# New emission orders for four stages of a convolution and attention kernel

## The chip, the cores and the metric

The kernel runs on one core of one Trainium2 chip. The metric is device time in microseconds (us) of one execution of the whole program; the time of a kernel is the median over several runs. A core has a matrix engine (TensorE, PE in the profile; its weight loads have a row of their own, PEld), a vector engine (DVE), a scalar engine (ACT), a further engine for simple fills (POOL), and an engine that here only issues transfers (SP). Each works through its own list of instructions in order, and waits at an instruction until its inputs and its output buffer are there. PSUM is the memory that PE writes; results are copied from it to SBUF by ACT or DVE.

## The reference

Four residual layers act on x, which has 2048 rows (positions) and 512 columns (channels), in bf16:

```python
x = A_u
x = x + _A_ref(_layernorm(x), A_re, A_im, B_re, B_im, C_re, C_im, log_dt, Dskip)
x = x + _B_ref(_layernorm(x), B_wqkv, B_wo)
x = x + _A_ref(_layernorm(x), ...)      # the same parameters again
x = x + _B_ref(_layernorm(x), B_wqkv, B_wo)
```

Layer A is a long convolution along the positions, one filter K per channel. K comes from a state-space model with 128 states n, and the convolution is done by Fourier transforms of twice the length:

```python
P = exp(logdA[:, :, None] * l[None, None, :])          # logdA = exp(log_dt) * (A_re + i A_im)
K = einsum("dn,dnl,dn->dl", Cc, P, dB).real            # dB = exp(log_dt) * (B_re + i B_im)
y = irfft(rfft(u padded) * rfft(K padded))[:L] + u * Dskip
```

Layer B is attention in a window: 32 heads of width 16, and each position looks at itself and at the 7 positions 2, 4, ... 14 before it:

```python
q, k, v = split(x @ wqkv)
logits = einsum("bhsd,bhswd->bhsw", q, k[idx]) * Dh ** -0.5     # w = 0..7, idx = pos - 2 w
o = einsum("bhsw,bhswd->bhsd", softmax(logits masked), v[idx])
return o @ wo
```

## The kernel before

The program runs in five stages, one for each entry of a list ORDERS: **prepare** (parameters, first layer norm), **first conv** (builds the filters and applies them), **B1** (first attention layer), **A2** (second convolution), **B2** (second attention layer).

**How a stage is ordered.** A stage doesn't emit its instructions at once. It records operations in a Plan, each with the engine it is for (P for PE, A for ACT, V for DVE, S for SP, G for POOL), a planner's duration, a function that emits the instructions, and the operations that must be emitted before it. Some steps exist in several ways, of which one is used (`either`): a sum on DVE, or by two identity matmuls on PE and a copy on ACT; a copy out of PSUM on ACT or on DVE (`moved`, lines 324 to 326); a transpose by DMA or on PE. `Plan.run` then emits the operations in the order of the numbers in ORDERS, taken as written, and a way is used if its numbers stand there:

```python
order = [int(i) for i in ORDERS[Plan.turn].split()]
Plan.turn += 1
taken = {self.ops[i][2] for i in order}
...
for i in order:
    fn, after, way = self.ops[i]
    fn()
```

So the numbers decide two things: for each engine the order in which it meets its work, and for some steps the engine. The planner's durations and due times were used where the numbers came from; nothing at run time reads them. The whole program is emitted under a manual schedule, so that nothing reorders it later.

**First conv, filters.** Channels are handled in 8 head groups (hc 0 to 7) for the filters and 4 channel blocks (dc 0 to 3, two head groups each) for the transforms. For a head group, DVE builds a table T of powers by doubling: at each level it multiplies the table by two multipliers (L386, L391, L392), and adds the two products. The sums of the larger levels are done on DVE (L399, L413) or on PE with ACT (matmuls L431 and L432, copy L436). The upper half of the table is made likewise (L407, L408: products; level 4: sum). Then three products with further factors (L456) give the right-hand sides: y0 and y1 in T's free parts, y2 in a tile of its own, Y2. PE contracts table and right-hand sides over the states (L469, L472: 256 matmuls for a head group, in eight pieces of 32), the result goes out of PSUM by ACT or DVE (L804) into KTq, to DRAM (k_scratch) and back in another layout (KT).

**First conv, transforms.** For the filters (kind k) and for the input (kind u), PE does the first Fourier step (L840), ACT copies it to Z (L845), Z is transposed to zt in four parts by DMA on SP's queue (or on PE, L871), PE does the second step (L860 to L863), and ACT copies the spectrum out (L867; tiles sp_u, sp_k). DVE multiplies the two spectra (L931, L932, tiles pa and pb); the halves are either joined on DVE (L936, L937), and then the inverse step has 8 matmuls, or not, and then it has 16 (L951 to L955). The result goes to VT by ACT or DVE (L959). A last step (L981) and a copy (L985) write the block of X. Filter spectra are stored for A2 (kt_scratch), also on SP's queue.

Buffers: T 2, Y2 1, pa and pb 2 each, zt and KTq together 4, spectra 8 of kind u and 4 of kind k, Z 1, and 3 for the PSUM tiles of sums and transforms, 2 for the contraction. An operation that takes the next buffer waits for the last reader of the one that it reuses.

**B1 and B2.** Norm and transpose of X (L153, xnT), projections to q and k (PE L1324; copies to qT and kT by ACT or DVE, L1329) and to v (L1344, L1349). For each of the 8 offsets, DVE multiplies qT with a shifted kT (L1375) and PE adds up each head with a matrix of ones (L1385). After the softmax DVE multiplies shifted values with the weights (L1487) and PE adds the offsets up with identity matmuls (L1503, L1508). The outcome is copied by ACT or DVE (L1523; L1525 for the last) and transposed. The output projection (L1560) is added to X either by DVE (L1543) or by an identity matmul ahead of it on PE (L1558) and a copy on ACT (L1656 with row sums, L1658 without). In B1 the next layer norm follows, with squares (L1664), a root (L174) and scaling (L1668, or L193 on DVE).

**A2** is first conv without the filters; spectra come back from kt_scratch.

Of the kernel before, what the change touches and what calls it, by code (L numbers as in the profile page):

```python
# [195 lines left out]
def load_params(nc, pp, prm):  # L196
# [13 lines left out]


ORDERS = [
    "297 1 3 2 7 5 8 21 9 25 10 20 24 22 11 12 225 15 13 29 229 26 14 27 33 233 31 23 41 34 237 44 46 37 43 50 249 47 "
    "51 231 38 58 245 60 57 235 61 48 241 298 59 227 68 299 72 74 253 239 77 300 75 84 251 69 88 85 90 247 99 303 76 "
    "91 98 243 304 106 104 307 255 114 107 115 308 120 136 320 124 258 256 132 259 137 125 108 109 257 92 139 93 260 "
    "138 261 122 321 123 146 262 154 156 263 158 133 291 152 293 279 269 159 287 155 276 301 168 166 164 302 322 169 "
    "167 174 323 175 182 184 305 180 324 306 185 325 183 191 190 311 200 201 309 207 198 196 310 312 206 199 264 313 "
    "212 219 317 218 213 314 272 326 288 282 315 294 266 274 327 284 316 270 280 328 141 296 140 147 319 318",
    "3 12 9 10 13 4 6 7 34 25 14 26 0 36 50 51 52 53 29 47 56 27 55 57 28 19 58 41 59 48 60 45 63 62 43 134 46 17 44 "
    "32 18 64 49 22 33 102 23 111 65 88 103 89 90 66 108 112 67 105 91 109 68 133 94 95 69 106 92 70 118 73 96 97 128 "  # L220
    "98 168 100 169 75 170 135 77 171 76 113 172 78 173 85 121 79 131 122 132 123 174 83 81 86 84 116 82 117 136 140 "
    "137 175 142 87 141 138 143 126 139 178 193 194 195 127 144 196 199 197 200 201 149 202 179 190 154 184 147 203 "
    "244 205 148 315 152 245 191 164 188 153 159 157 189 165 186 158 246 187 166 206 247 192 162 283 163 248 292 269 "
    "207 284 270 167 286 249 271 293 230 289 272 314 287 275 209 250 273 232 290 214 212 299 251 210 305 236 222 276 "
    "306 277 309 278 216 254 234 279 349 281 307 316 220 218 350 255 224 308 266 302 226 260 228 312 294 303 238 313 "
    "267 241 239 242 317 261 321 318 319 268 322 323 324 297 320 351 374 375 376 298 352 325 377 380 353 381 378 354 "
    "330 355 335 356 382 359 383 384 328 429 386 500 329 333 430 431 340 363 387 334 338 345 364 432 346 395 389 339 "
    "433 347 365 361 393 391 343 362 397 434 344 371 348 372 369 399 401 367 370 468 368 474 475 471 373 469 472 477 "
    "435 454 499 478 455 456 457 460 403 489 458 461 462 436 494 404 439 479 463 406 464 534 466 411 409 441 501 407 "
    "443 535 442 536 492 444 537 451 413 493 484 538 445 482 417 415 497 483 419 539 498 452 447 420 449 448 502 450 "  # L230
    "504 540 503 422 453 505 506 423 487 507 541 508 562 428 509 563 564 565 568 488 510 569 544 570 566 520 427 525 "
    "571 545 572 574 513 556 617 550 514 515 523 524 530 528 557 532 529 551 533 618 558 622 619 620 623 559 624 621 "
    "638 575 625 639 640 641 626 518 561 642 650 519 576 560 531 578 651 632 579 583 581 644 645 633 646 629 599 585 "
    "630 426 636 647 600 589 653 648 591 602 587 654 425 663 603 605 592 634 665 594 635 676 656 597 637 666 596 657 "
    "677 607 667 684 669 608 610 685 670 614 659 613 611 679 660 615 672 616 682 662 680 687 692 673 688 700 675 694 "
    "690 701 696 703 698 705 706 717 708 718 711 709 714 712 715",
    "58 1 59 39 2 3 20 40 4 41 21 60 11 10 22 7 23 5 16 24 13 26 17 42 28 32 43 14 47 194 30 61 49 35 104 68 195 62 "
    "66 79 64 105 54 45 76 81 75 101 78 197 102 51 82 199 72 85 84 107 86 228 110 108 229 112 113 244 88 115 248 245 "
    "89 119 246 249 230 120 247 94 232 122 252 233 231 250 123 96 253 234 124 251 97 91 236 254 235 92 237 116 256 "
    "258 257 255 118 259 163 242 240 98 164 238 241 100 243 239 144 260 132 145 264 262 133 278 263 265 126 274 284 "  # L240
    "279 127 135 285 275 272 136 160 129 286 161 266 273 130 138 287 268 267 139 154 288 147 269 276 155 151 289 157 "
    "270 152 277 290 159 271 291 169 280 296 179 170 332 172 176 180 340 185 177 333 334 186 341 182 338 335 183 191 "
    "200 344 339 192 148 346 345 149 188 336 347 189 141 342 201 337 142 166 297 343 167 173 348 305 298 174 301 350 "
    "306 351 365 302 352 379 366 282 205 353 283 307 380 206 202 319 354 367 308 203 355 320 368 356 214 321 357 369 "
    "217 215 299 370 218 358 211 359 300 375 212 208 364 376 373 209 220 226 223 303 221 227 374 224 311 304 309 312 "
    "385 310 377 313 316 393 315 378 386 395 318 394 399 396 389 400 322 390 371 323 372 397 381 324 383 387 398 384 "
    "391 325 388 429 326 392 430 331 404 407 401 406 415 408 403 413 416 409 414 431 410 419 523 432 411 420 524 433 "
    "521 417 434 412 421 522 418 437 438 422 439 440 527 423 441 525 426 442 425 448 528 443 452 526 428 449 456 497 "
    "529 450 531 453 446 533 457 454 532 451 444 447 530 455 463 534 461 498 445 535 465 462 464 536 473 541 466 459 "
    "501 543 469 537 474 460 475 503 467 502 471 539 470 472 504 479 476 468 493 480 477 499 485 489 481 494 500 490 "  # L250
    "491 486 549 505 483 508 487 507 484 550 545 509 562 488 506 546 492 482 510 553 564 561 495 511 563 589 512 565 "
    "554 517 590 566 595 572 519 604 567 591 513 605 574 608 571 596 516 586 606 610 597 587 569 619 559 588 618 621 "
    "607 560 620 609 622 573 611 612 623 575 613 624 576 616 626 577 614 578 628 581 579",
    "0 5 1 14 15 2 7 8 9 4 10 6 12 11 3 13 17 21 105 109 18 23 106 25 111 29 26 33 31 113 34 117 121 114 119 37 39 "
    "123 38 193 197 45 195 48 199 201 42 49 205 202 51 124 59 206 52 133 60 81 62 53 208 82 70 55 63 217 57 281 84 71 "
    "64 127 282 73 136 68 285 211 67 137 169 85 286 220 214 74 170 139 86 130 221 75 172 90 147 88 140 79 289 78 148 "
    "141 173 290 101 144 174 145 150 102 158 176 179 95 151 159 293 223 96 152 294 161 98 154 296 242 156 224 99 92 "
    "162 243 253 93 245 225 254 302 163 246 229 227 305 256 231 165 167 308 299 232 257 247 309 234 258 251 311 249 "
    "330 262 260 341 235 331 312 180 342 333 319 181 186 320 334 236 187 189 344 240 183 190 239 313 184 345 264 322 "
    "317 346 315 265 323 276 350 267 272 348 277 324 273 335 328 279 326 268 337 339 269 275 361 358 362 355 359 271 "  # L260
    "352 356 353",
    "1 20 2 3 58 21 4 22 59 39 12 8 9 23 60 40 16 5 24 13 26 17 41 30 32 42 61 14 28 194 62 68 35 43 101 64 195 45 66 "
    "104 102 49 51 47 79 105 54 76 80 126 77 75 85 127 72 82 86 107 83 228 88 108 229 90 91 230 110 92 232 94 112 244 "
    "231 233 113 96 236 97 245 114 119 234 248 237 120 235 246 249 116 122 250 252 247 117 251 242 98 240 243 99 253 "
# [1462 lines left out]
```

## Time and profile before

| what | us |
|---|---|
| five runs | 517.34, 518.18, 519.84, 521.27, 521.65 |
| median | 519.84 |
| the profiled execution | 521.86 |
| its span (first to last instruction) | 520.1 |
| prepare / first conv / B1 / A2 / B2, by where the tiles of one end and the next begin | 57 / 162 / 123 / 48 / 130 |
| granted clock of PE, mean | 0.962 |

The page of the profile gives busy time of each engine, slices of the span (a digit is a busy share in tenths), the DMA queues, the chain of work that ended last, and groups of like instructions. A row of a group has the line in the kernel, the engine, the operation, output and input tiles with their shapes, the count, busy time and the mean of one in ns, and the idle time just before them with what ended it. The view of busy time by stretches has for each stretch its length, then busy time and instruction count for PE, weight loads, DVE, ACT and POOL, then PE's granted clock, the share of time that the DMA engines were busy, and GB/s. The view of waits sums, for an engine at a tile and line, what it waited for: total, number, longest. "issue" there means that nothing which the profile shows held the instruction back. The timeline lists start, duration, instruction, and in brackets idle time ahead of it and what ended it.

### The profile page before, as it was taken

What the parts mean: (1) busy time and instruction counts of PE and PEld (TensorE: products, weight loads), DVE (VectorE), ACT (ScalarE), POOL (GpSimd) and SP (SyncE); (2) the same over time, 40 slices, a digit from 0 to 9 for tenths busy, and PEclk for the clock granted to TensorE, in tenths of its full rate; (3) what the DMA queues carried; (4) which work ended last, traced back from release to release, by engine and by line L of the source; (5) the groups of instructions that cost most, each with busy time, mean ns of one, the idle gap of its engine ahead of it and who ended that gap; (6) DMA issues with size and microseconds to landing.
All of it is one profiled execution on the core that took longest, in us unless ns stands there. A gap on an engine that the chain in (4) does not pass through costs nothing.

```text
span 520.1 us, 12435 instructions
## 1 busy us (share of the span) xinstructions
PE 419.2 (81%) x5208; PEld 245.4 (47%) x5224; DVE 474.9 (91%) x808; ACT 326.3 (63%) x482; POOL 13.0 (3%) x63
## 2 busy tenths in 40 slices
PE   1600678689778879899999879879997999998896
PEld 1500554367455548543355434556674434563353
DVE  6999999979997999789999999889999498999995
ACT  4999677658575758742655336989996546551320
POOL 0000000000000002200000000000000000000000
PEclk9999998979897969999999999989999999999999
DMA  8940464664664362651010622479510700203233
GB/s 258 164 169 1 82 115 112 126 131 94 116 141 114 52 155 68 202 106 47 16 59 28 112 40 40 113 253 182 71 36 0 122 30 20 83 24 88 42 75 148
DMA packets 105389, 49.87 MB, mean 96 GB/s; under 512 B 90619, under 2 KB 97532, under 8 KB 105076
## 3 DMA queue, kind: packets, MB, share of 16 engines
q1 hardware_dynamic: 104900, 48.67, 41.9%
q8 instruction: 41, 0.67, 0.5%
q10 hardware_dynamic: 432, 0.39, 0.2%
q14 instruction: 16, 0.13, 0.1%
HBM read 15.78 MB, written 8.13 MB: 46 GB/s over the span
## 4 chain that ended last, share of the span: by engine, by line
PE 40%; DVE 30%; ACT 11%; issue 8%; DMA 7%; SPq 4%; POOL 0%; DVEq 0%; ACTq 0%
PE ps_qk L1324 11%; DVE prod L1487 5%; PE ps_v L1344 5%; PE Lp L1385 4%; DMA zt<-Z 3%; DVE ln_st_b L153 3%; SPq L646 3%; DVE Ttab L456 2%; DVE Y2tab L456 2%; DVE prod L1375 2%; ACT Z L845 2%; PE psk L469 2%; DVE Ttab L392 2%; PE ps_o L1560 2%; PE po L1503 2%
## 5 line engine op out<-in xcount | busy, mean ns | idle before, releaser
L1375 DVE TENSOR_TENSOR prod<-qT,kT 128x2048 bf16<-128x2048 bf16 (+1 forms) x80 | 76.8, 1005 | 7.5 <-ACT kT L1329 6.0
L1487 DVE TENSOR_TENSOR prod<-VX,L 128x2048 bf16<-128x2048 bf16 (+2 forms) x96 | 77.3, 860 | 1.2 <-PE po L1508 0.7
L1324 PE MATMUL ps_qk<-xnT,wqk 128*128 128x512 bf16 x256 | 62.6, 382 | 0.0
L1503 PE MATMUL po<-prod,sb_ident 128*128 128x512 bf16 x215 | 54.7, 379 | 4.8 <-DVE prod L1487 2.9
L1324 PEld LDWEIGHTS <-wqk 128*128 128x128 bf16 x256 | 22.3, 98 | 30.9 <-issue 10.2
L1503 PEld LDWEIGHTS <-sb_ident 128*128 128x128 bf16 x224 | 21.0, 97 | 32.7 <-issue 9.0
L840 PE MATMUL ps_s<-X,sb_F 128*128 128x128 bf16 x128 | 12.2, 259 | 27.4 <-ACT X L669 25.5
L1344 PE MATMUL ps_v<-wv,xnT 128*128 128x256 bf16 x256 | 33.0, 278 | 1.2 <-ACT xnT L1302 1.0
L840 PEld LDWEIGHTS <-sb_F 128*128 128x128 bf16 x256 | 17.2, 108 | 33.7 <-issue 25.8
L1385 PE MATMUL Lp<-prod,sb_bones 128*32 128x512 bf16 x256 | 28.3, 388 | 4.6 <-DVE prod L1375 4.6
L456 DVE TENSOR_TENSOR Ttab<-Ttab,MPA 128x2048 bf16<-128x2048 bf16 (+2 forms) x20 | 28.4, 1433 | 3.0 <-ACT Ttab L436 2.8
L472 PE MATMUL psk<-Y2tab,Ttab 128*32 128x48 bf16 x1024 | 22.3, 199 | 10.2 <-issue 9.7
L845 ACT CAST Z<-ps_s 128x1024 bf16<-128x1024 f32 (+1 forms) x32 | 28.9, 996 | 1.7 <-DMA zt<-Z 0.9
L1349 ACT CAST VX<-ps_v 128x512 bf16<-128x512 f32 x31 | 18.2, 586 | 18.1 <-PE ps_v L1344 18.1
L1344 PEld LDWEIGHTS <-xnT 128*128 128x128 bf16 x256 | 24.0, 99 | 9.2 <-issue 4.0
L1560 PE MATMUL ps_o<-wo_t,oT 128*128 128x512 bf16 x108 | 27.7, 379 | 0.5 <-DVE X L1543 0.2
L456 DVE TENSOR_TENSOR Y2tab<-Ttab,MPB 128x6144 bf16<-128x6144 bf16 (+1 forms) x13 | 27.2, 2118 | 0.3 <-PE psk L472 0.3
L1523 ACT CAST ot<-po 128x1024 bf16<-128x1024 f32 x13 | 12.6, 1015 | 23.1 <-PE po L1503 21.1
L469 PE MATMUL psk<-Ttab 128*32 128x64 bf16 x1024 | 22.6, 204 | 5.3 <-DVE Ttab L456 2.8
L472 PEld LDWEIGHTS <-Ttab 128*32 128x32 bf16 x1024 | 19.8, 99 | 13.0 <-issue 12.8
L1329 ACT CAST kT<-ps_qk 128x512 bf16<-128x512 f32 x25 | 14.6, 585 | 16.8 <-PE ps_qk L1324 16.8
L153 DVE BATCH_NORM_STATS2 ln_st_b<-X 128x6 f32<-128x128 bf16 (+2 forms) x80 | 22.9, 354 | 2.1 <-ACT X L985 2.1
(231 smaller groups left out, 1031.3 us busy)
## 6 DMA issues: line engine op xcount, KB each, us to landing
X<-in_A_u_dram SPq DMA_DIRECT2D x8, 512.0 KB, 5.7
kt_scratch<-sp_k SPq DMA_DIRECT2D x16, 256.0 KB, 3.6
Kt<-kt_scratch SPq DMA_DIRECT2D x16, 256.0 KB, 6.3
out_dram<-X SPq DMA_DIRECT2D x4, 512.0 KB, 2.7
k_scratch<-KTq SPq DMA_DIRECT2D x7, 256.0 KB, 2.7
KT<-k_scratch SPq DMA_DIRECT2D x7, 256.0 KB, 2.9
VX<-VX SPq DMA_DIRECT2D x4, 448.0 KB, 3.8
kT<-kT SPq DMA_DIRECT2D x8, 192.0 KB, 2.1
```

What stands on the lines that cost most here:

```text
L153: self.nc.vector.bn_stats(self.st[:, j, part, :], X[:, j, a:b])
L456: nc.vector.tensor_tensor(d, src.to_broadcast([128, c, n, 2 * EYB]), mm.to_broadcast([128, c * n, EYB, 2]), ALU.mult)
L469: nc.tensor.matmul(o.rearrange("e (s i) -> e s i", s=2), xs, T[:, 1:3, h, m // 2, :, t], start=(m == 0), stop=False, skip_group_check=True)
L472: nc.tensor.matmul(o[:, EYB:].rearrange("e (q i) -> e q i", q=3), xs, Y2[:, :, h, 1 - m // 2, :, t], start=False, stop=(m == 3), skip_grou ...
L845: nc.scalar.copy(box["Z", kind, dc][:, 0:n // 8, :, jq * 32:(jq + 1) * 32].rearrange("p g r k -> p r g k"), box.pop(("s1", kind, dc, jq))[ ...
L1324: nc.tensor.matmul(ps[:], wqk[:, ct, f0:f0 + 128], xnT[:, 4 * s:4 * s + 4, ct, :], start=(ct == 0), stop=(ct == 3))
L1344: nc.tensor.matmul(ps[:, jj].rearrange("p t h d -> p (t h d)"), xnT[:, j + jj, ct, :], wv[:, ct, fp * 256:(fp + 1) * 256], start=(ct == 0) ...
L1375: nc.vector.tensor_tensor(pr[:, 0:n2], qT[fp][:, a:a + n2, j0 * 128:j0 * 128 + 1024], kT[fp][:, a:a + n2, c0:c0 + 1024], ALU.mult)
L1385: nc.tensor.matmul(Lp[r0:r0 + 32, w // 4, :], bones[:, w % 4, :], pr[:, f2 - a, hb * 512:(hb + 1) * 512], start=(n == 1), stop=(n == 4), s ...
L1487: nc.vector.tensor_tensor(p2[:, 0:nj].rearrange("p j t d h -> p (j t) d h"), VX[:, fp, NV + a:NV + a + nj].rearrange("p j (t d h) -> p (j ...
L1503: nc.tensor.matmul(po[:, c:c + 512], ident[:], p2[:, k + j:k + j + 2].rearrange("p j t d h -> p (j t d h)"), start=(n == 1), stop=(n == W))
L1560: nc.tensor.matmul(ps, box["oT"][:, ft // 2, j, ft % 2, :], wo_t[:, ft, :], start=(ft == 0 and not res), stop=(ft == 3))
```

## The change

Only the first four entries of ORDERS are replaced: those of prepare, first conv, B1 and A2. No function changes, no tile, no pool; the entry of B2 stays. Both kernels record the same operations under the same numbers, so an order that names other numbers takes another way.

```diff
 ORDERS = [
-    "297 1 3 2 7 5 8 21 9 25 10 20 24 22 11 12 225 15 13 29 229 26 14 27 33 233 31 23 41 34 237 44 46 37 43 50 249 47 "
...
+    "297 1 3 2 7 5 8 20 9 25 10 21 24 22 11 12 225 15 13 29 229 26 14 27 33 237 31 23 41 34 233 44 46 37 43 50 253 47 "
...
-    "3 12 9 10 13 4 6 7 34 25 14 26 0 36 50 51 52 53 29 47 56 27 55 57 28 19 58 41 59 48 60 45 63 62 43 134 46 17 44 "
...
-    "137 175 142 87 141 138 143 126 139 178 193 194 195 127 144 196 199 197 200 201 149 202 179 190 154 184 147 203 "
-    "244 205 148 315 152 245 191 164 188 153 159 157 189 165 186 158 246 187 166 206 247 192 162 283 163 248 292 269 "
...
+    "3 9 6 10 4 7 39 12 40 37 13 38 34 0 41 50 14 51 52 53 56 54 57 29 58 59 47 24 42 49 60 168 62 48 134 17 32 18 19 "
...
+    "81 84 154 82 144 246 87 149 159 157 247 248 193 158 194 249 195 196 250 199 166 197 200 147 222 152 148 251 162 "
+    "153 164 206 201 163 202 165 254 208 167 203 349 205 315 283 350 210 255 286 316 284 351 287 266 212 289 352 260 "
...
```

In words, the numbers come to this.

| stage | what changes engine | what changes place |
|---|---|---|
| prepare | nothing | a few neighbouring copies and products swap |
| first conv | two table sums of 128x2048 from PE and ACT to DVE, that is 16 fewer matmuls L431/L432 and 4 fewer copies L436; two pairs of joins from DVE to longer inverse steps (8 more matmuls each of L953 and L954); of KTq one copy and of its last part (KTu) one from DVE to ACT, of VT one from ACT to DVE | head group 3 is built before 2 (before: 2, then 3); contractions are emitted in pieces between transforms; the products of channel blocks 0, 1 and 2 go 2,0,3,1 / 3,0,2,1 / 2,0,1,3 (before 0,3,1,2 / 0,1,2,3 / 0,1,3,2); the four transposes of a filter spectrum are issued ahead of its stores |
| B1 | four copies to kT (L1329), one copy to ot (L1523) and one copy-like residual step each for two row blocks (L1543, replaced by L1558 and L1658) from DVE to PE and ACT; one norm from ACT to DVE | the first row blocks' statistics and projections, some products |
| A2 | one copy of VT from DVE to ACT | a few copies |

At channel block 0 the order of first conv is now as follows, in the numbers of the diff: 154, 144, 149, 159 are the four transposes of the filter spectrum on SP; 157, 147, 152, 162 the second Fourier steps of these parts on PE, and 158, 148, 153, 163 their copies on ACT; 193 to 196 and 199 to 202 the eight pieces of the contraction of head group 2 on PE, of which six stand between 157 and 147; 222, 206 and later 230, 214 the products on DVE; 208 the inverse step of the second of them. Before, 144, 149, 154 came first, the stores 164 and later 165, 166 among them and 159 behind 164, and the eight pieces stood ahead of 147.

## The prediction

> **What bounds the kernel now.** I read the page first, then busy time by stage, then the waits, then the instructions around the longest waits. The page says which engines can set the end:
>
> ```profile
> span 520.1 us, 12435 instructions
> PE 419.2 (81%) x5208; PEld 245.4 (47%) x5224; DVE 474.9 (91%) x808; ACT 326.3 (63%) x482; POOL 13.0 (3%) x63
> ...
> PEclk9999998979897969999999999989999999999999
> ...
> q8 instruction: 41, 0.67, 0.5%
> ```
>
> DVE (VectorE) is busy 474.9 of 520.1 us, so only 45 us in the whole span can be won without taking work off it. Queue q8 brings TensorE's instructions: 10,432 of them in 41 packets of 16 KB, one packet for about 254.
>
> The stages in one row each (length; busy us and instruction count of PE, weight loads, DVE, ACT, POOL; granted clock; DMA share; GB/s). They are prepare, first conv, first attention layer (B1), second conv (A2), second attention layer (B2):
>
> ```profile
> 0.00:57.25 57.25, 15.20 (x368) 12.55 (x368) 52.79 (x102) 49.32 (x79) 0.75 (x10) 1.00 0.55 134
> 57.25:219.00 161.75, 130.82 (x2926) 87.70 (x2928) 148.44 (x208) 108.89 (x139) 7.47 (x13) 0.91 0.56 121
> 219.00:342.00 123.00, 112.51 (x739) 54.86 (x746) 113.86 (x207) 67.81 (x117) 2.39 (x20) 1.00 0.31 70
> 342.00:390.00 48.00, 44.66 (x413) 32.50 (x411) 44.39 (x93) 44.48 (x67) 0.00 (x0) 0.96 0.61 120
> 390.00:520.10 130.10, 116.01 (x772) 57.80 (x776) 115.44 (x202) 55.76 (x83) 2.39 (x20) 0.98 0.26 63
> ```
>
> In the first conv DVE leads clearly (148.4 of 161.75, so 13.3 idle); PE and ACT have 31 and 53 us to spare, and only their lateness at a hand-over costs anything. In B1 DVE and PE are level. In A2 three engines lie within 0.3. The waits (engine, tile, line, what released it; total, times, longest):
>
> ```profile
> PE psk L472 <- issue: 9.7, 4, 3.9
> PE xp L860 <- DMA zt<-Z: 6.1, 3, 3.9
> ...
> DVE pa L931 <- PE vp L955: 3.0, 2, 2.5
> ...
> DVE Ttab L456 <- ACT Ttab L436: 2.8, 1, 2.8
> ...
> DVE pa L931 <- ACT sp_k L867: 1.9, 3, 0.9
> ```
>
> The three DVE rows are the visible cost, 7.7 us, and the PE rows are where they begin:
>
> ```profile
> 135.38 0.20 PE L472 MATMUL psk<-Y2tab,Ttab 128*32 128x48 bf16 x3 [2.26 <-issue]
> ...
> 137.30 0.63 PE L862 MATMUL xp<-zt,sb_C 128*128 128x512 bf16 x1
> ```
> ```profile
> 157.89 0.23 PE L472 MATMUL psk<-Y2tab,Ttab 128*32 128x48 bf16 x4 [3.94 <-issue]
> ```
> ```profile
> 163.53 1.23 DVE L456 TENSOR_TENSOR Ttab<-Ttab,MPA 128x2048 bf16<-128x2048 bf16 x1 [2.83 <-ACT Ttab L436]
> ```
>
> PE stands 3.94 us inside a contraction with nothing to wait for but instructions; the sums queued behind it finish late; ACT's copy L436 is late; DVE waits 2.83.
>
> **The change, part by part.** Only emission orders of four stages move; counts below are from the orders of the two kernels.
>
> *Prepare.* Same operations on the same engines, neighbours swapped. DVE is busy 52.79 of 57.25 and waits at the start for loads that do not move: 0 (bounds -1 to +1).
>
> *First conv, work.* Two more sums of 128x2048 (L399, 1.22 us each) on DVE: +2.4. Two pairs of joins L936/L937 (0.42 each) leave it for longer inverse matmuls: -1.7. Copies: two fewer of KT halves, one more VT (0.69): -0.7. DVE net 0.0. PE loses 16 sum matmuls and gains 16 of 128x256 (-16x0.43+16x0.27 = -2.6); ACT loses four copies L436 (1.02 each) and nets one KT copy: -3.5. Neither pays directly with 31 and 53 us spare.
>
> *First conv, waits removed.* I counted the DVE work standing between a PE/ACT sum's last input and DVE's first use of its result, in start-to-start times of the same instructions in the trace (1.14 for a 128x2048 one whose row says 1.22). Before, the shortest are 2.14 and 2.33 us, and those two gave 0.43 and 2.83. After, the shortest is 3.46, and the one nearest to a late contraction has more than 4. A sum takes 8x0.21 on PE and 2x1.02 on ACT, partly overlapped, about 3.0; so they should vanish: -3.3. Two waits of spectrum products for their spectra (0.92, 0.35), one for Y2 (0.34) and the product wait behind the 3.90 us transpose (2.53) also stand at places that the new order undoes: -4.1. Gone: 7.4.
>
> *First conv, waits added.* (a) The first spectrum product of channel block 0 follows the issue of its DMA transposes after 5.41 us of DVE work. Before, 6.11 and 5.92 gave waits of 0.92 and 0.35. So 0.9 to 1.6: 1.2. What is late next: the inverse matmuls, then pa's buffer. (b) The second product's transform stands on PE behind six of eight contraction pieces. With one fetch gap of 2 us its cover of 7.2 falls short by 0.8 to 2.8: 1.8. (c) PE itself waits for the first transpose: its landing takes 4.1 us (median of 42) plus the issue, DVE's work in between is only 2.85, so PE idles 1.3 to 3; behind it on PE stand the pieces of contraction 2 and the other transforms, for which ACT's copies and DVE's products wait, which is (a) and (b). [...] In the trace, after the 2.26 us gap at 135.38 the 128x512 matmuls start every 0.43 instead of 0.21 us until 139.0, and the granted clock of 130 to 140 is 0.83. [...] By the row, 8 matmuls at +0.21 follow it: 1.7, of which I take 0.7, since contraction pieces, which run at the pace of fetches, stand between. [...] (d) Products write two buffers of pa; one product of the last block stands 2.62 us behind the one whose buffer it reuses, with 4.3 needed: 1.7 (before, 3.28 against 3.57 gave 0.51). (e) Y2 has one buffer. The table of head group 5 is written directly when DVE reaches it, 7.45 us after contraction 4 may begin; that takes 4.0 to 4.7 and its fetch gap 0 to 3.9: wait 0 to 1.2, I take 0.6. DMA issues on SP keep their number; the k transposes now go out ahead of the stores of the kernel spectrum, which were hidden. POOL's fills of the tables follow their table and POOL is busy 7.5 of 161.75: 0. Added: 6.0. First conv: -7.4 + 6.0 = -1.4; bounds -6 (fetches fall well) and +5.
>
> *B1.* Four casts L1329 (0.69) go to ACT, where one takes 0.585; DVE is 27.5 busy of 33 us there (229 to 262) while PE is at 32.45, so PE hides most: of 2.8 I take -0.9, for the cast at the head of DVE's stretch and part of the product waits. One cast L1523 (1.22) goes to ACT (1.0), and two residual sums L1543 (0.68) become PE identity matmuls (0.38) and ACT copies (0.57); one norm of 0.40 comes to DVE. From 262 to 327 DVE is 62.71 of 65 busy and every microsecond counts, but from 327 to 342 ACT is 13.86 of 15, PE 14.12, DVE 13.73, and ACT takes up to 2.1 more. Of 2.2 I take -1.0. B1: -1.9; bounds -4.6 (all of DVE's saving) and +2.1 (ACT's tail on the path).
>
> *A2.* One VT copy goes from DVE (0.69) to ACT (0.60) with DVE, ACT and PE level: 0, bounds -1 and +1. *B2.* Same order: 0; it only starts earlier or later.
>
> Sum: -1.4 - 1.9 = -3.3. The profiled run took 521.86 us, span 520.1 plus 1.8 around it: it would become 518.6. It lies 2.0 above the median of the five runs, 519.84; I carry the difference over: 516.5.
>
> **Rivals.** *Full gain:* contractions spread between transforms give the fetches time, (b), (c) and (e) vanish (-3.1), and B1 gives its -3: 516.5 - 3.1 - 1.1 = 512.3. For: contraction pieces now alternate with transforms, which issue slower. Against: a contraction has two fetches whatever the order.
>
> *Nothing in B1, half in the conv:* PE paces B1 (112.51 against 113.86 tells how little), its tail gives back the rest, the conv gives -0.7: 519.1. That the orders don't matter, since data dependencies rule, ends here too; against it stand waits that the order alone makes.
>
> *Slower: the fetch in contraction 2.* The second product of block 0 hangs on a transform behind six pieces of that contraction. If a 3.94 us fetch gap falls there rather than 2, and the transforms that follow run at half clock (four of four matmuls, 16x0.21 = 3.4, not 0.7), its wait is 1.8 + 1.9 + 2.7 = 6.4; the pa buffer and Y2, whose covers are short or nil, pass it on instead of absorbing it, about 2 more. +6.6 on 516.5: 523.1. For: the 157.89 row did just this with a cover of 2.33. Against: 7.2 of cover. It decides once PE comes 5.9 us later than in my sum (519.84 + 2.6 - 516.5).
>
> **How the numbers follow.** A measurement of this kernel tells about 0.5%, 2.6 us. Chances: my case 0.40, full gain 0.13, no change 0.13, slower 0.34 (it has the largest single price, and new short covers tend to come where a count like mine doesn't look). Mine spans 513.5 to 519.5: of its 0.40, 0.29 is faster, 0.09 same, 0.02 slower. So faster 0.42, same 0.22, slower 0.36. Likeliest 516.5; 8 in 10 from 511.5 to 526.5, the lower end just past the full gain, the upper one past the slower rival by the +3.4 left of its bounds.
>
> **What would show it.** DVE's busy time falls by 4 to 6 us, nearly all in B1. The 2.83 and 2.53 waits are gone; waits of 0.9 to 2 stand at the products of block 0 and one in the last block; Y2's wait is at most 1.2. B1 is 1 to 3 us shorter, A2 and B2 within 1. Wrong: a first conv longer than 164 us, or DVE waits for PE of over 3 us in it; B1 no shorter though DVE is less busy in it; B2 different by over 2 us.

## The result: 0.6% faster, and not where the sum had it

| kernel | median us | runs | profiled execution us (span) |
|---|---|---|---|
| before | 519.22 | 76 | 521.86 (520.1) |
| changed | 515.74 | 41 | 513.88 (512.1) |

The ratio is 0.9939 with a 95% interval of 0.9926 to 0.9952, which is -3.2 us, or -2.5 to -3.8. The prediction's sum was -3.3. The two profiled executions stand 8.0 us apart, because that of before lies above its median and that of the changed kernel below: one profile of each doesn't give the size, and second profiles of both were taken with the experiments.

From the page of the changed kernel:

```profile
span 512.1 us, 12435 instructions
PE 409.8 (80%) x5211; PEld 239.2 (47%) x5226; DVE 469.3 (92%) x798; ACT 327.5 (64%) x486; POOL 13.0 (3%) x63
...
q8 instruction: 41, 0.67, 0.6%
```

DVE is busy 5.6 us less, as forecast (4 to 6); 4.0 of it is in B1, where nearly all was expected, 0.7 in first conv and 1.0 in A2. The stages, with their ends moved to the same work as before (columns as before):

```profile
57.25:211.70 154.45, 120.87 (x2931) 83.41 (x2930) 147.72 (x205) 105.86 (x135) 7.49 (x13) 0.96 0.58 127
211.70:334.90 123.20, 113.50 (x735) 54.59 (x741) 109.82 (x204) 71.47 (x124) 2.39 (x20) 1.00 0.30 74
334.90:382.10 47.20, 43.92 (x418) 31.40 (x418) 43.34 (x89) 45.04 (x68) 0.00 (x0) 1.00 0.59 110
382.10:512.10 130.00, 115.74 (x769) 57.61 (x774) 115.38 (x202) 55.63 (x83) 2.39 (x20) 0.98 0.26 63
```

First conv is 154.45 us long where it was 161.75, with 0.7 us less DVE work: it lost waits. B1 is 123.2 where it was 123.0, although DVE is busy 4.0 us less in it (109.82 after 113.86): what left DVE there came back as waiting. The waits say the same:

```profile
PE xp L860 <- DMA zt<-Z: 7.1, 6, 3.2
...
PE psk L469 <- issue: 6.0, 3, 2.6
PE psk L472 <- issue: 5.0, 2, 2.5
...
DVE prod L1375 <- ACT qT L1329: 4.2, 1, 4.2
...
DVE pa L931 <- ACT KTu L1009: 2.0, 1, 2.0
```

The rows for sums (L456 on L436) and for inverse steps (L931 on vp) are gone, so DVE lost 5.8 us of waits there and got one of 2.0. TensorE's instruction stalls are not gone: 11.0 us by these two rows, against 12.3 us of such gaps before. In B1 one wait of 4.2 us for qT is new.

### The profile page after: what moved, and what is told of

It reads as the page before. It is cut to its first block, busy times and chain, and to the rows that moved or that the text cites. A ratio compares the mean times of both kernels' runs of the same rounds, so it can differ in the third digit from the quotient of the medians.

```text
span 512.1 us, 12435 instructions
## 1 busy us (share of the span) xinstructions
PE 409.8 (80%) x5211; PEld 239.2 (47%) x5226; DVE 469.3 (92%) x798; ACT 327.5 (64%) x486; POOL 13.0 (3%) x63
## 4 chain that ended last, share of the span: by engine, by line
DVE 41%; PE 32%; ACT 9%; issue 8%; DMA 5%; SPq 3%; POOL 0%; DVEq 0%; ACTq 0%
PE ps_qk L1324 11%; PE ps_v L1344 5%; DVE prod L1487 4%; DVE Ttab L456 4%; DVE Y2tab L456 4%; PE Lp L1385 4%; DVE ln_st_b L153 3%; DVE Ttab L392 3%; DVE Ttab L399 3%; SPq L646 3%; DVE Ttab L391 2%; DVE prod L1375 2%; PE po L1503 2%; DVE Ttab L408 2%; DVE Ttab L407 1%
## 5 line engine op out<-in xcount | busy, mean ns | idle before, releaser
L840 PEld LDWEIGHTS <-sb_F 128*128 128x128 bf16 x256 | 16.9, 108 | 31.8 <-issue 24.5
L840 PE MATMUL ps_s<-X,sb_F 128*128 128x128 bf16 x128 | 10.8, 241 | 26.2 <-ACT X L669 24.7
L1523 ACT CAST ot<-po 128x1024 bf16<-128x1024 f32 x14 | 13.6, 1015 | 26.0 <-PE po L1503 26.0
L456 DVE TENSOR_TENSOR Ttab<-Ttab,MPA 128x2048 bf16<-128x2048 bf16 (+2 forms) x20 | 28.4, 1433 | 0.2
L1329 ACT CAST kT<-ps_qk 128x512 bf16<-128x512 f32 x29 | 17.0, 585 | 17.8 <-PE ps_qk L1324 17.8
L456 DVE TENSOR_TENSOR Y2tab<-Ttab,MPB 128x6144 bf16<-128x6144 bf16 (+1 forms) x13 | 27.2, 2120 | 0.0
L469 PEld LDWEIGHTS <-Ttab 128*32 128x32 bf16 x1024 | 19.1, 100 | 16.4 <-issue 15.6
L472 PE MATMUL psk<-Y2tab,Ttab 128*32 128x48 bf16 x1024 | 21.2, 197 | 5.2 <-issue 5.0
```

The source lines that it names most:

```text
L456: nc.vector.tensor_tensor(d, src.to_broadcast([128, c, n, 2 * EYB]), mm.to_broadcast([128, c * n, EYB, 2]), ALU.mult)
L469: nc.tensor.matmul(o.rearrange("e (s i) -> e s i", s=2), xs, T[:, 1:3, h, m // 2, :, t], start=(m == 0), stop=False, skip_group_check=True)
L840: nc.tensor.matmul(o, F1[:, j, r, :], rhs(j), start=True, stop=not dk)
```

## Experiments

The expectations name two theories: P is the sum of the prediction, C is what the two profiles suggest. All intervals are against the kernel before on the same chip. "Stage end" below is the start of B1's own first statistics, which wait for one of the last four copies of X out of first conv; "rest" is from there to the end.

### Which stage's order pays

Only the first two strings of ORDERS are the new ones (x1_conv):

```diff
-    "297 1 3 2 7 5 8 21 9 25 10 20 24 22 11 12 225 15 13 29 229 26 14 27 33 233 31 23 41 34 237 44 46 37 43 50 249 47 "
...
+    "297 1 3 2 7 5 8 20 9 25 10 21 24 22 11 12 225 15 13 29 229 26 14 27 33 237 31 23 41 34 233 44 46 37 43 50 253 47 "
...
-    "3 12 9 10 13 4 6 7 34 25 14 26 0 36 50 51 52 53 29 47 56 27 55 57 28 19 58 41 59 48 60 45 63 62 43 134 46 17 44 "
...
+    "3 9 6 10 4 7 39 12 40 37 13 38 34 0 41 50 14 51 52 53 56 54 57 29 58 59 47 24 42 49 60 168 62 48 134 17 32 18 19 "
...
```

> New orders of prepare and first conv, old orders of B1 and A2. Theory P (the sum of the prediction): -1.4 us against the kernel before. Theory C (the profiles: first conv carries all, B1 gives nothing because TensorE paces its head): the whole difference of the medians, -3.0 to -3.7 us, and a first conv without DVE waits above 0.5 us between 60 and 195 us.

Only the third string is new (x2_b1); prepare, first conv and A2 keep their old ones:

```diff
-    "58 1 59 39 2 3 20 40 4 41 21 60 11 10 22 7 23 5 16 24 13 26 17 42 28 32 43 14 47 194 30 61 49 35 104 68 195 62 "
...
+    "39 58 40 1 59 20 2 3 41 21 60 4 42 22 12 7 5 23 9 13 24 16 26 14 28 32 30 47 17 197 43 45 35 49 104 61 199 66 "
...
```

> New order of B1 alone. Theory P: -1.9 us. Theory C: within 0.5 us of the kernel before; DVE is busy about 4 us less in B1 and waits about 4 us more, in one wait of over 3 us at the first product of queries and keys.

The first two strings and the fourth are new, B1's is old (x3_conv_a2):

```diff
-    "0 5 1 14 15 2 7 8 9 4 10 6 12 11 3 13 17 21 105 109 18 23 106 25 111 29 26 33 31 113 34 117 121 114 119 37 39 "
...
+    "5 1 0 9 4 10 3 2 13 6 15 7 11 14 12 8 17 21 105 109 18 23 106 25 111 26 29 33 30 35 113 117 39 114 121 119 37 "
...
```

> New orders of prepare, first conv and A2, old order of B1. Theory P: the changed kernel without B1's gain, so 1.9 us slower than it and -1.4 us against before. Theory C: as fast as the changed kernel within 0.6 us, -3.0 to -4.3 us against before.

The changed kernel again, and in the next round the kernel before again, without an edit:

> The changed kernel once more, for a second profile of it beside the others. Theory C: -3.5 us against before; the span of the second profile lies within 3 us of 512.1 and first conv again shows no wait of DVE for sums. If the profiled pair's 8.0 us came from one odd execution of the changed kernel, the span is near 516 and waits of 1 us or more are back in first conv.

> The kernel before once more, for a second profile. If the profiled pair (span 520.1 against 512.1) overstates the change because the profiled execution of before was a slow one, this span is 515 to 518 and its waits for sums (2.83 us) and for the inverse step (2.53 us) are smaller or elsewhere; if they belong to the order, they are there again at the same instructions within 1 us.

And, after these, B1 and A2 both new behind the old first conv (z1_b1_a2), that is, the third and the fourth string:

> Old orders of prepare and first conv, new orders of B1 and A2. B1's new order alone came out 3.3 us slower. If its cost is real and its own, this is 1 to 4 us slower than before, and the time from the first statistics of B1 to the end is 301.5 to 303.5 us in the profile (old orders: 299.8 to 301.2). If A2's new order was made to follow it and pays it back, 0 within 1 us. Theory P: -1.9 us.

| kernel | median us (before beside it) | ratio, 95% interval | stage end | rest |
|---|---|---|---|---|
| before, first profile | | | 218.9 | 301.2 |
| before, second (y1) | 517.96 (519.09) | 0.9983, 0.9950 to 1.0015 | 216.2 | 299.8 |
| changed, first profile | 515.74 (519.22) | 0.9939, 0.9926 to 0.9952 | 211.6 | 300.5 |
| changed, second (x4) | 515.78 (518.97) | 0.9939, 0.9910 to 0.9968 | 212.5 | 303.3 |
| first conv new (x1) | 515.63 (518.97) | 0.9953, 0.9923 to 0.9982 | 212.1 | 301.7 |
| first conv and A2 new (x3) | 516.54 (518.97) | 0.9970, 0.9942 to 0.9998 | 212.2 | 301.9 |
| B1 new (x2) | 522.63 (518.97) | 1.0063, 1.0031 to 1.0096 | 219.6 | 302.2 |
| B1 and A2 new (z1) | 523.47 (519.36) | 1.0073, 1.0047 to 1.0098 | 220.1 | 301.9 |

First conv's new order carries the gain. By the median x1 is within 0.2 us of the changed kernel, as theory C has it. The times alone don't decide: x1's interval (-0.9 to -4.0 us) also holds theory P's -1.4, and x3 (-1.6, from -0.1 to -3.0) fits P as well. The traces do. No DVE wait above 0.3 us stands in x1's first conv before one of 1.40 at 195.4 us, and with the new order the stage ends at 211.6 to 212.5 us, with the old one at 216.2 to 220.1. The second profile of the changed kernel has a longer span than expected, 515.7 us; its first conv is nearly as short as in the first, 212.5 us.

B1's new order gives nothing: with the new first conv the rest is 300.5 and 303.3 us, against 301.7 and 301.9 with B1's old order. Behind the old first conv it even costs 3.3 and 3.8 us in two kernels, and most of that is the seam between two strings that were not made for each other. The end of first conv's string says in which order the last four parts of X are copied out: parts 3, 0, 1, 2 (numbers 718, 709, 712, 715) in the old one, 2, 3, 1, 0 in the new one. B1's string begins with the statistics of part 3 (number 58) in the old one, of part 2 (39) in the new one. So in the kernel before, as in the changed one, DVE starts after the first of the four copies; with B1 alone new it starts after the fourth:

```profile
218.24 1.91 ACT L985 CAST X<-ps_y 128x512 bf16<-128x512 f32 x3 [0.69 <-PE ps_y L981]
218.86 0.87 DVE L153 BATCH_NORM_STATS2 ln_st_b<-X 128x6 f32<-128x128 bf16 x4 [1.93 <-ACT X L985]
```
```profile
217.00 2.57 ACT L985 CAST X<-ps_y 128x512 bf16<-128x512 f32 x4 [0.69 <-PE ps_y L981]
219.60 0.87 DVE L153 BATCH_NORM_STATS2 ln_st_b<-X 128x6 f32<-128x128 bf16 x4 [3.92 <-ACT X L985]
```

That is 2.0 us more of waiting (3.92 for 1.93) in x2 and z1, and 0.7 (2.60) in x1 and x3, where DVE starts after the second copy. Less these 2.0 us, the old first conv ends at 217.6 and 218.1 us in x2 and z1, inside the 216.2 to 218.9 of before: it is not longer. The other 1.3 and 1.8 us agree with the rest, which is about 1.5 us longer than in the two profiles of before (300.5 on average). A2's new order, in z1, doesn't pay it back.

The second profile of before has the same two large waits at the same instructions as the first (2.53 and 2.83 us there), so they belong to the order:

```profile
112.54 0.69 DVE L931 TENSOR_TENSOR pa<-sp_u,sp_k 128x1024 bf16<-128x1024 bf16 x1 [2.22 <-PE vp L955]
```
```profile
161.14 1.23 DVE L456 TENSOR_TENSOR Ttab<-Ttab,MPA 128x2048 bf16<-128x2048 bf16 x1 [2.45 <-ACT Ttab L436]
```

By the two profiles of each kernel, first conv is 5.5 us shorter and the rest 1.4 longer, together -4.1 beside -3.5 by the medians.

### Taking one wait away

In the kernel before, the one sum in front of the 2.83 us wait is made on DVE (440) instead of by two steps on PE (441, 443) and two copies on ACT (442, 444); operations between these are left out here:

```diff
 # first conv, head group 6, level 3
-439 441 443 442 444 451
+439 440 451
```

> The kernel before with one sum of head group 6 (level 3, the one with 2.33 us of DVE work between its inputs and its use) made on DVE instead of TensorE and ACT, in the place where DVE waited for it. Cover theory: the wait of 2.83 us goes, 1.14 us of DVE work comes, -1.7 us. Rival (the wait is only where some slack of the stage shows, and comes back elsewhere): 0 to +1.2 us.

Measured: ratio 1.0006, interval 0.9984 to 1.0027; the rival's value. The wait is gone and the stage ends at 217.6, inside the range of the old order. A new wait of 0.88 us (for X) stands at 173.6, and one for a filter spectrum at 193.4 is 1.04 us, where the first profile of before has 0.60. Removing the largest wait of the list, one place alone, was worth nothing that could be measured.

### Does the new order stand lateness better?

> The kernel before with 64 matmuls of each of the eight contractions issued twice (the first of an accumulation, started anew, so the values stay): 128 instructions more, about 1.3 us of TensorE's issue time for each contraction, 10 us in all, in a stage where TensorE has 31 us to spare. Cover theory: this kernel, with covers of 2.1 to 3.3 us at its sums and products, loses 4 to 10 us.

> The changed kernel with the same doubled matmuls. Cover theory: with covers of 3.5 us and more it takes part of the lateness, loses 1 to 4 us, and stands 5 us or more ahead of the other one. If the new order merely moved work off TensorE or lost its stalls, both lose alike (difference within 1.5 us of 3.5).

```diff
 # Tables.contract
+if m == 0:
+    nc.tensor.matmul(o.rearrange("e (s i) -> e s i", s=2), xs, T[:, 1:3, h, 0, :, t],
+                     start=True, stop=False, skip_group_check=True)
 if m % 2 == 0:
     nc.tensor.matmul(o.rearrange("e (s i) -> e s i", s=2), xs, T[:, 1:3, h, m // 2, :, t],
```

Before with the extra matmuls: 526.06 us, ratio 1.014 (1.008 to 1.020). Changed with them: 527.16, ratio 1.0183 (1.0133 to 1.0233). The old order lost 1.4% (7 us, as expected), the changed one 2.4% of before's time (over 11 us, where 1 to 4 were expected), and its lead was gone. That speaks against longer covers as what the change brought: an order that stood lateness better would have kept its lead. But the edit also adds 1,024 instructions, 128 for each contraction, which by the step of 256 between stalls (last section) move the later fetches, and so these two runs don't separate lateness from the places of fetches.

### Moving the fetches and nothing else

The last test leaves both orders as they are and moves the places in TensorE's list at which a new block of instructions begins. 64 tiny matmuls are started twice in prepare, at a time when TensorE waits for other engines (18.8 us ahead of its first L840 in the first profile of before); with their weight loads that is 128 instructions, half a block of 256 (the step between stalls in the table of the last section):

```diff
 # prepare, sums of the rows of X
 for j in (j2 * 2, j2 * 2 + 1):
+    for _ in range(8 if j2 < 4 else 0):
+        nc.tensor.matmul(rows[:, j:j + 1], xT[:, j, 0, :], ones[:, 0:1], start=True, stop=False, skip_group_check=True)
     for ct in range(4):
         nc.tensor.matmul(rows[:, j:j + 1], xT[:, j, ct, :], ones[:, 0:1], start=(ct == 0), stop=(ct == 3), skip_group_check=True)
```

> The kernel before with 64 tiny matmuls (128 instructions with their weight loads, half of one fetch) started twice in prepare, where TensorE waits 22 us for other engines. Nothing moves but the places in TensorE's list at which a new fetch begins. If stalls of fetching set the waits of first conv (the 3.9 us one inside a contraction ahead of the 2.8 us wait of DVE), stalls move to other instructions and the time changes by 1.5 us or more, most likely down. If the order alone sets them: within 1 us of before, the same waits at the same instructions.

> The changed kernel with the same 128 instructions more in prepare. If the new order is good because its fetches fall where DVE does not wait, it loses 1.5 to 4 us here, and waits of DVE come back in first conv. If its gain is of the order alone: within 1 us of the changed kernel, -2.5 to -4 us against before.

| kernel | median us (before beside it) | ratio, 95% interval | stage end | rest |
|---|---|---|---|---|
| before, shifted (z3) | 519.12 (519.36) | 0.9993, 0.9970 to 1.0016 | 217.5 | 301.3 |
| changed, shifted (z4) | 519.81 (519.36) | 1.0009, 0.9983 to 1.0035 | 218.3 | 301.7 |

The changed kernel lost the whole gain, 0.7%, to 128 instructions that cost nothing where they stand: the rest is unchanged and first conv ends 6 to 7 us later. The old order kept its time. Its expectation, 1.5 us or more if stalls set the waits, was missed, yet its waits moved: that for the inverse step is 0.36 us (2.53 in the first profile of before), that for the sum 1.96 (2.83), and one for a filter spectrum grew from 0.60 to 2.19. So a shift moves waits in both orders, and only in the changed one did the total change. One shift was tried; one by a whole block, which by that step should move no boundary, was not.

In the trace of the shifted changed kernel the waits for sums and inverse steps are still gone, but others have come. TensorE stalls inside the contraction of head group 2, and the transforms behind it run at half clock (granted 0.50, one matmul every 0.43 us; these lines stand two lower than in the kernel, L862 for L860):

```profile
109.05 0.22 PE L472 MATMUL psk<-Y2tab,Ttab 128*32 128x48 bf16 x1 [2.68 <-issue]
...
110.31 0.63 PE L864 MATMUL xp<-zt,sb_C 128*128 128x512 bf16 x1
110.74 0.63 PE L865 MATMUL xp<-zt,sb_C 128*128 128x512 bf16 x1
```
```profile
112.45 0.69 DVE L933 TENSOR_TENSOR pa<-sp_u,sp_k 128x1024 bf16<-128x1024 bf16 x1 [3.37 <-ACT sp_k L869]
```

The product that waits 3.37 us is the second of channel block 0, the one of which the prediction said that its transform stands behind six pieces of that contraction. In the first profile of the changed kernel as it is, no stall falls there, and the same product starts without a wait, with the one in front of it:

```profile
107.38 0.69 DVE L931 TENSOR_TENSOR pa<-sp_u,sp_k 128x1024 bf16<-128x1024 bf16 x1
...
109.22 0.69 DVE L931 TENSOR_TENSOR pa<-sp_u,sp_k 128x1024 bf16<-128x1024 bf16 x1
```

The last wait of the stage, for KTu, also grew from 2.0 to 4.2 us in the shifted kernel.

### B1's tail

> The changed kernel with B1's last row blocks as before: residual sums of blocks 10 and 13 on DVE again, three norms on the engines that they had. If ACT's tail of B1 takes back what DVE saved (the bound of +2.1 us), this is 0.5 to 2 us faster than the changed kernel, -4 to -5.5 us against before, and DVE's waits for row sums near the end of B1 (1.2 and 1.3 us) shrink. If not, it is as fast as the changed kernel or 1.4 us slower.

```diff
 # B1: residual sums of row blocks 10 and 13, norms of 9, 13 and 14
-555 556   592 593 594   570 617 625
+553 554   589 590 591   571 616 626
```

Measured: ratio 0.9943 (0.9921 to 0.9965), against 0.9939: as fast as the changed kernel. The rest is 302.7 us. The edit also gives DVE its work back, so the equal time doesn't tell whether ACT's tail takes back what DVE saves or neither counts. Of DVE's two waits for row sums near the end (1.16 and 1.30 us in the second profile of the changed kernel) one shrank to 0.63, the other is 1.30 as before, and a new one of 1.09 us stands behind them.

## Why the prediction was right, and where it was not

The change was put at -3.3 us and is -3.2 by the ratio (515.7 for 516.5, since more runs put the kernel before at 519.2, not 519.8), by two errors that cancel: that the sum came out is luck. One of its own signs of being wrong came true, B1 no shorter though DVE is less busy in it. By the prediction's own steps:

**First conv, waits removed (-7.4).** Right. All listed waits are gone in both profiles of the changed kernel; those for sums and for the inverse step are gone in the shifted one too. The second profile of before has the two large ones again, 4.7 us together, and the small ones below 0.3 us, so 7.4 was the upper end of what an execution pays.

**First conv, waits added (+6.0).** This is the step that failed. (a), (b) and (e) cost DVE nothing: no wait above 0.3 us stands in it between 57 and 195 us. (d), 1.7 us in the last block, came as 2.0 and 2.2 us, though behind ACT's copies of KTu and a spectrum rather than behind pa's buffer, so its size was right by chance. The chain of (a) to (c) shows how the rest was mis-sized:

```profile
100.00 5.39 SPq L854 DMA_TRANSPOSE zt<-Z  x4
```
```profile
103.31 0.39 PE L860 MATMUL xp<-zt,sb_C 128*128 128x512 bf16 x1 [3.17 <-DMA zt<-Z]
```

The transposes went out at 100.00, when ACT had the last part of Z ready. The prediction counted DVE's work from the place of the transposes in the order, 5.41 us; counted from when they ran it is 107.38 - 100.00 = 7.4 us. The place in the order only says what stands ahead on the same queue; SP and ACT were ahead of DVE. TensorE did wait as (c) said, 3.17 us, a little over the 1.3 to 3 given, and that too cost DVE nothing. For (b) one fetch gap of 2 us was assumed in the contraction; the built order has none there. Put there by the shift, it gives 3.4 us of wait, more than the 1.8 of (b). So the shifted kernel did what the rival "the fetch in contraction 2" describes (a stall of 2.68 us inside that contraction, transforms at a clock of 0.50 behind it), and which of the two cases came about was decided, in the two builds run, by the position of TensorE's instructions in blocks of 256, which the prediction did not count. The rival's own size was high: it put the slow case at 523.1, and the shifted kernel is at 519.8.

**The clock.** What the row at 135.38 showed behind a gap of 2.26 us came again in the changed kernel: behind the 3.17 us gap the first two matmuls of 128x512 last 0.39 and 0.38 us, the next two 0.58 and 0.63, and the granted clock between 100 and 110 us is 0.83. In the shifted kernel a gap of 2.66 us, for a transpose, came first, and the clock was at half before the fetch stall began:

```profile
102.53 0.39 PE L862 MATMUL xp<-zt,sb_C 128*128 128x512 bf16 x1 [2.66 <-DMA zt<-Z]
```
```profile
101.00:104.80 3.80, 1.48 (x61) 0.84 (x63) 3.77 (x6) 1.08 (x2) 0.00 (x0) 1.00 0.99 187
104.80:106.50 1.70, 1.57 (x134) 1.41 (x119) 1.63 (x4) 0.55 (x1) 0.00 (x0) 0.50 1.13 280
```

It stayed at 0.50 up to 115 us, so the 3.4 us of wait there hold both the stall and slow transforms. The 0.7 us taken for the clock was not paid in the changed kernel, since DVE was not waiting there.

**B1 (-1.9).** Wrong: it gave nothing. The four casts were taken as worth 0.9 us. They are worth nothing because TensorE's projections pace the head of the stage: from the first statistics to the first product takes 15.6 us in both profiles of before and 15.7 in both of the changed kernel (16.9 and 16.6 with B1 new behind the old first conv). TensorE runs without a gap from 219.24 to 228.3 us, and what DVE no longer does it now waits:

```profile
219.24 1.05 PE L1344 MATMUL ps_v<-wv,xnT 128*128 128x256 bf16 x8 [0.66 <-ACT xnT L1302]
220.15 2.96 PE L1324 MATMUL ps_qk<-xnT,wqk 128*128 128x512 bf16 x12
222.94 1.04 PE L1344 MATMUL ps_v<-wv,xnT 128*128 128x256 bf16 x8
223.82 4.48 PE L1324 MATMUL ps_qk<-xnT,wqk 128*128 128x512 bf16 x20
```
```profile
227.23 0.69 DVE L1375 TENSOR_TENSOR prod<-qT,kT 128x1024 bf16<-128x1024 bf16 x1 [4.23 <-ACT qT L1329]
```

The other 1.0 us, from the copy and the sums at the end, did not come either; putting the sums back changed nothing. Later waits of DVE are longer too: that for the sums of a softmax on TensorE is 1.94 us instead of 0.80, and one of 1.31 us for row sums from ACT is new. Which of these would have to go for B1 to end earlier is open.

**A2 and B2 (0).** A2's new order, x3 against x1 (516.54 and 515.63, overlapping intervals), shows no gain. B2 lasts 124.4 to 125.4 us from A2's last copy on in all profiles of unshifted kernels.

## What to carry to other kernels

An order's gain can hang on something that no wait names: here 128 instructions early in TensorE's list, where it had time to spare, took a gain of 0.7% away. Before costing a reorder of many small matmuls, count the instructions into fetch blocks (256 each in these traces) and see in which bursts TensorE passes two block boundaries soon after each other (1.28 and 1.72 us in two cases with a stall, 4.15 in one without, by the last table), and test a tuned order by padding before relying on it. Test the orders of neighbouring stages together as well as alone: swapping one string cost up to 2.0 us at the seam. And measure slack from the time at which the producer ran in the trace, not from its place in the emission list; where another engine set the pace, work taken away turned into waiting of about the same length (DVE in B1: 4.0 us less work, one wait of 4.2 us more).

## What was not expected of the hardware

TensorE's stalls sit on a grid. Counted over matmuls and weight loads in order of start, the stalls of first conv of about 0.5 us and more that end with "issue" begin at these instructions (first profiles):

| kernel | instruction number (us of stall) |
|---|---|
| before | 1212 (0.5), 1724 (1.4), 2490 (2.0), 3768 (2.3), 4534 (3.9), 5302 (2.1) |
| changed | 1212 (2.6), 1724 (2.6), 2234 (2.4), 3768 (1.0), 5302 (2.3) |
| changed, shifted | 1212 (3.3), 1724 (3.2), 2490 (2.3), 3002 (2.7), 3768 (0.7), 4024 (1.7), 5302 (1.4), 5558 (2.0), 6324 (1.6) |

The distances are multiples of 256, but for one to three instructions; counted with the semaphore and drain records of TensorE's queue (37 in the profile of before, 34 in that of the changed kernel) those of the first two rows are exact multiples. The fetches are in the traces too, as the packets of queue q8: 41 of 16 KB in the changed kernel, one for about 255 of its 10,437 matmuls and weight loads. In all 14 profiles taken, each of the 98 stalls between 57 and 220 us that last 0.5 us or more and end with "issue" ends 1.2 to 1.7 us after such a packet has landed. Three cases (us):

| kernel | passes a boundary | packet begins, lands | reaches the next boundary | goes on |
|---|---|---|---|---|
| before, ahead of the 2.83 us wait | 152.67 | 155.42, 156.54 | 153.95 | 157.89 |
| changed, shifted, contraction of head group 2 | 104.65 | 106.00, 107.55 | 106.37 | 109.05 |
| changed, the same two boundaries | 105.85 | 106.72, 108.45 | 110.0 | 110.0 |

So TensorE stalled where it passed a whole block in 1.28 and 1.72 us, before the next packet had landed, and not where it took 4.15 us; over the stalls of 0.9 us and more in six profiles, from one boundary to the first instruction after the next took 2.5 to 5.2 us. In the changed kernel the three transforms among the contraction's pieces took the time: it came to the boundary 1.5 us after the packet had landed, which is not later than stalls end elsewhere, so it had little or nothing to spare. Whether a stall costs the kernel anything then depends on what is queued behind it: 11 us of stalls remain in the changed kernel, at places for which DVE doesn't wait.
